# First batch's queries and keys loaded and turned in two token parts, with a new hand-written order, in an attention and channel-mix kernel

## The chip, the cores and the metric

One core of a Trainium2 chip runs the whole kernel in one launch. The metric is the device time of one execution in microseconds (us). A run's time is the time of the whole execution; the profiler's span, from the first to the last instruction, is some 2 us shorter.

## What is computed

Eight batches of 576 tokens. First, attention with 8 heads of 64 dimensions and a causal mask over blocks of 64 tokens; then, on its output `x` (576 tokens by 512 channels), a channel mix:

```
scores = q @ k^T / 8, kept where block(i) >= block(j)      # block = token // 64
x      = softmax(scores) @ v                               # heads side by side: 512 channels
xk     = mu_k * x + (1 - mu_k) * x_prev                    # x_prev: x one token earlier, 0 at the first
xr     = mu_r * x + (1 - mu_r) * x_prev
kk     = max(xk @ w_k, 0)                                  # 512 -> 1024
out    = sigmoid(xr @ w_r) * ((kk * kk) @ w_v)             # 1024 -> 512
```

Inputs and output are float32; the products run in 16 bits with float32 sums.

## The kernel before

**Tasks and order.** The kernel first lists all its work as tasks (`plan.add`): each names its engine, its inputs and the ring buffers that it uses. Then it issues them in the order of a list of task numbers, `ORDER` (line 15). Each engine works through its own tasks in that order and waits where an input isn't there or a buffer isn't free. Where a task may run on several engines, a letter of `PLACE` (line 53) says which: P for GpSimd (POOL), D for VectorE (DVE), A for ScalarE (ACT). A number with `+n` puts n "unread" products ahead of a TensorE (PE) task: 128x512 products whose result nobody reads (`unread`, line 218). A PSUM tile is taken from a ring of four (`ps`), and the queries and keys land in a ring of four tiles (`nb`).

**Queries and keys.** `add_qk` (line 235) loads, for a batch b and a pair half g, the queries (n = 0) or keys (n = 1) of four heads as one 128-partition tile: 288 KB after the conversion to bf16 that the DMA makes. The DMAs are issued from POOL's queue (line 249), two per tile in batches 0 and 1 (64 partitions each), one per tile from batch 2 on. VectorE then turns the tile with one transpose (line 260).

**Scores and exponentials.** `add_unit` (line 349) makes a group of score products `sc` (line 365), 8 to 32 small products of 32 rows by 64 columns, and the exponential of them on ScalarE, `ex` (line 386). In batches 0 and 1 a group is cut in two halves of heads: half 0 needs only g = 0, half 1 only g = 1.

**Batch 0 goes by tokens.** Its scores are made for tokens 0 to 255 (groups "00", "01") and for 256 to 575 ("10" to "14"); `add_part` (line 506) makes for each part the row sums (`sum`, line 524), their reciprocals (lines 405 to 419), the products with the values (`av`, line 544) and the normalised x (`norm`, line 556). The loads of batch 0 are whole all the same: a score of the first part waits for whole tiles.

**Values.** For batch 0 a one-column copy on ScalarE, `hold` (line 293), stands ahead of the loads of the values: it reads the first key tile and writes into the value tile, so that the value loads (line 284, half from SP's queue, half from ACT's) go out only when the first keys have landed. POOL converts the first value tile (line 214), then issues the weights' loads (line 324) and batch 1's queries and keys.

**Mix.** `add_mix` (line 572) makes for each of four channel groups the difference or scaled copy `d` (line 584, or 580 on ScalarE) and from it xk and xr with one VectorE instruction each, `mul` (lines 600 and 604). Then come the products `pk` with w_k (line 644), `pr` with w_r (line 687), `pv` with w_v (line 721), with `relu` and `sq` (lines 659 to 671), `tanh` (line 697), the output `o` (line 731) and its store (line 740). A chunk c is 512 tokens across the batches' borders.

**PE's order in batch 0:** 27 unread products; the seven half-0 score groups of both parts; the two half-1 groups of the first part; its `sum` and `av`; the five half-1 groups of the second part; 9 unread products; `sum` and the two `av` of the second part; then `pr` and `pk` of chunk 0, mixed with batch 1's scores.

Of the kernel before, what the change touches and what calls it, by code (L numbers as in the profile page):

```python
# [8 lines left out]
FP = mybir.dt.float32  # L9
# [3 lines left out]
ALU = mybir.AluOpType  # L13

ORDER = """
# [38 lines left out]
    "DDDDPDPAPADDAPPAADAADPPDDPAPDPAAPPDADAPPPDAADAPDDAPDPDPDPAADPAAAADPAAA"  # L54
    "AAAAADPDADPAADPAPAPAPDDDAADAADPDAAPAAAPADAPADAADPADAA")
# [56 lines left out]
def kernel(  # L112
# [60 lines left out]
    def new(buf):  # L173

        return slots[buf["ring"], buf["slot"]]
# [9 lines left out]
    MUS = consts.tile([P, 2, D], FP)  # L185
    MUT = consts.tile([P, 2, 2, RW], FP)
# [11 lines left out]
    SPLIT = (0, 1)  # L198
    HALVES = (0, 1)
# [35 lines left out]
    def add_qk(b, g, n):  # L235

        src, qkt = (q, k)[n], qkt_buf[b]
        nb = plan.buf("nb")  # L240

        def rows():
            return new(nb)

        def fetch(eng, me):
            parts = ([(D * y, D, GH * y + 2 * g, 2) for y in range(2)]
                     if b in HALVES else [(0, P, GH * g, GH)])
            for p0, np_, h0, nh in parts:
                nc.gpsimd.dma_start(
                    rows()[p0:p0 + np_],  # L250
                    src[b, h0:h0 + nh].rearrange(
                        "y (r j) d -> (y r) (j d)", j=TOK))
        t = add(f"qkld {b} {g} {n}", ("POOL",), fetch, uses=[nb], kind="ldc",
                kb=P * LW * 4 / 1024, starts=2 if b in HALVES else 1)

        if n:
            loads.setdefault(b, (nb, t))

        def turn(eng, me):
            nc.vector.transpose(  # L260
                new(qkt)[:, n, g].rearrange("p t e -> p (t e)").bitcast(
                    FP).rearrange("p (r j) -> p j r", r=RW),
                rows()[:, :].bitcast(FP).rearrange(
                    "p (j s) -> p j s", s=RW))
        evac["qkt", b, g, n] = add(f"turn {b} {g} {n}", ("DVE",), turn, [t],
                                   uses=[nb, qkt], kind="turn", cols=S)

# [70 lines left out]
    PARTS = [(0, 256), (256, 576)]  # L338
# [10 lines left out]
    def add_unit(b, name, pieces, split):  # L349
# [23 lines left out]
        for h in range(2):  # L373
            if split or not h:
                mine = (2 * h, 2 * h + 1) if split else range(GH)
                pe = add(f"sc {b} {name} {h}", ("PE",),
                         lambda eng, me, mine=mine: fn(eng, me, mine),
                         [evac["qkt", b, g, n]
                          for g in sorted({place(b, a, y)[0] for a in mine
                                           for y in range(2)})  # L380
                          for n in range(2)],
                         uses=([ms[h]] if split else ms) + [qkt_buf[b]],
                         kind="sc", cols=[n for _, _, _, n in pieces])
# [188 lines left out]
    def add_mix(b, cc, lo0, hi, xs):  # L572
# [16 lines left out]
        for n in range(2):  # L589
            buf = mix_buf[b][n]  # L590

            def mul(eng, me, n=n, buf=buf):
# [5 lines left out]
                e = nc.vector if eng == "DVE" else nc.gpsimd  # L598
                if sub["eng"] == "ACT":
                    e.scalar_tensor_tensor(  # L600
                        dst, x, MUT[:, n, cc % 2, cc // 2:cc // 2 + 1],
                        dt[:, n, 0:W], ALU.mult, ALU.add)
                else:
                    e.scalar_tensor_tensor(  # L604
                        dst, dt[:, 0, 0:W],
                        MU1[:, n, cc % 2, cc // 2:cc // 2 + 1], x,
                        ALU.mult, ALU.add)
            t = add(f"mul {b} {cc} {n} {lo0}",
                    ("DVE",), mul,
# [139 lines left out]
    add("spare", ("PE",), lambda eng, me: unread(me, new(wbuf)[:, 0]), uses=[wbuf],  # L749
# [84 lines left out]
```

## Time and profile before

| | |
|---|---|
| median of 3 runs | 260.37 us (259.85 to 262.7) |
| the profiled execution's own time | 262.33 us |
| its span | 260.2 us |
| PE busy | 242.6 us, 93% of the span |
| DVE, ACT, POOL busy | 73%, 62%, 31% |
| PE busy from 0 to 62 us | 49.39 us |
| PE busy from 100 to 250 us | 150.0 us |

How to read it. A line such as `L365` is a line of the kernel. In the timeline a row is: start, duration, engine, line, operation, result and source with their shape, count, and in brackets the idle time before it and what ended that. Rows of the same kind are merged, so the duration can contain short waits. "issue" stands for idle time in which the engine waited for nothing that the profile shows. The TensorE clock that was granted is given as a share of full speed. PE's ends are modelled, so a busy PE is not PE at its peak.

### The profile page before, as it was taken

To read this page: it belongs to the slowest core of one execution; us is meant where nothing else is said; L and a number is where in the kernel's file an instruction comes from. 1 tells how busy PE (TensorE), PEld (TensorE's weight loads), DVE (VectorE), ACT (ScalarE), POOL (GpSimd) and SP (SyncE) were. 2 spreads that over 40 slices of the span, in tenths; PEclk is the share of its full clock that TensorE was granted. 3 is DMA by queue.
4 is the path that set the end of the run, shared out by engine and by line. 5 is a ranking of instruction groups with operands and counts; after the bars stand their busy time and mean duration, and the time that the engine had idled before them with its cause. 6 is when DMAs were issued, how large, how long until landed. Compare 5 with 4: busy or idle time off the path is not lost.

```text
span 260.2 us, 8926 instructions
## 1 busy us (share of the span) xinstructions
PE 242.6 (93%) x4058; PEld 132.3 (51%) x4058; DVE 188.8 (73%) x233; ACT 162.4 (62%) x184; POOL 80.3 (31%) x88
## 2 busy tenths in 40 slices
PE   8859498879999999999999999999999999999994
PEld 3536356654454446644454487444554764444442
DVE  1737889597888699899688969884699389444322
ACT  1456048877656969796777786786887743274220
POOL 6074256841405610060455234420000221142000
PEclk9988989997999999999999999999999999999999
DMA  5999996899699995449785930021002200300224
GB/s 88 194 165 189 207 217 103 134 191 215 102 253 238 168 208 181 90 96 215 196 137 97 215 110 3 3 98 65 4 5 81 83 5 12 150 3 0 81 82 161
DMA packets 49189, 31.50 MB, mean 121 GB/s; under 512 B 38528, under 2 KB 39808, under 8 KB 49152
## 3 DMA queue, kind: packets, MB, share of 16 engines
q1 hardware_dynamic: 40128, 18.29, 29.7%
q0 software_dynamic: 6688, 12.06, 27.6%
q10 hardware_dynamic: 2336, 0.59, 1.5%
q8 instruction: 31, 0.51, 0.8%
q14 instruction: 6, 0.05, 0.1%
HBM read 33.56 MB, written 9.44 MB: 165 GB/s over the span
## 4 chain that ended last, share of the span: by engine, by line
PE 84%; DMA 6%; ACT 3%; issue 3%; DVE 1%; POOL 0%; ACTq 0%; DVEq 0%; POOLq 0%
PE t_ps L644 25%; PE t_ps L721 23%; PE t_ps L687 12%; PE t_ps L365 10%; PE t_ps L460 8%; PE t_ps L449 4%; DMA t_lv<-in_v_dram 4%; ACT t_e L386 2%; PE t_ps L544 2%; DMA t_nb<-in_k_dram 1%; DMA out_dram<-t_o 1%; PE t_ps L222 1%; DVE t_o L731 1%; PE t_ps L524 1%; ACT L293 0%
## 5 line engine op out<-in xcount | busy, mean ns | idle before, releaser
L386 ACT ACTIVATE t_e<-t_ps 128x1024 f16<-128x1024 f32 (+4 forms) x98 | 87.6, 957 | 30.9 <-PE t_ps L365 30.1
L644 PE MATMUL t_ps<-t_xk,WK 128*128 128x512 f16 (+3 forms) x416 | 66.9, 314 | 0.4 <-ACT t_e L386 0.3
L721 PE MATMUL t_ps<-WV,t_k 128*128 128x512 f16 (+1 forms) x296 | 64.6, 374 | 0.0
L671 POOL TENSOR_TENSOR t_k<-t_kr 128x1024 f16<-128x1024 f32 x16 | 30.5, 1907 | 76.9 <-DVE t_kr L661 62.5
L644 PEld LDWEIGHTS <-WK 128*128 128x128 f16 x416 | 37.0, 98 | 26.1 <-issue 2.4
L721 PEld LDWEIGHTS <-t_k 128*128 128x128 f16 x296 | 28.1, 98 | 33.1 <-issue 1.9
L365 PE MATMUL t_ps<-t_qkt 32*64 32x64 bf16 (+7 forms) x1344 | 37.3, 290 | 6.1 <-ACT t_e L386 3.8
L260 DVE STREAM_TRANSPOSE t_qkt<-t_nb 128x576 f32<-128x576 f32 x32 | 38.1, 1242 | 1.5 <-PE t_ps L365 1.0
L697 ACT ACTIVATE t_t<-t_ps 128x1024 f32<-128x1024 f32 x18 | 18.5, 1028 | 31.5 <-PE t_ps L687 31.5
L687 PE MATMUL t_ps<-WR,t_xr 128*128 128x512 f16 x144 | 35.1, 390 | 0.4 <-ACT t_e L386 0.4
L659 ACT ACTIVATE t_kr<-t_ps 128x1024 f32<-128x1024 f32 x22 | 22.4, 1024 | 18.8 <-PE t_ps L644 18.3
L365 PEld LDWEIGHTS <-t_qkt 32*64 32x64 bf16 x1344 | 21.8, 106 | 22.9 <-issue 17.9
L731 DVE SCALAR_TENSOR_TENSOR t_o<-t_t,t_ps 128x1024 f32<-128x1024 f32 (+2 forms) x20 | 22.1, 1108 | 14.9 <-PE t_ps L721 9.9
L661 DVE TENSOR_SCALAR t_kr<-t_ps 128x1024 f32<-128x1024 f32 x14 | 17.1, 1224 | 19.5 <-PE t_ps L644 19.4
L584 POOL TENSOR_TENSOR t_d<-t_xt 128x576 f32<-128x576 f32 (+2 forms) x10 | 11.6, 1162 | 36.3 <-DVE t_xk L604 13.5
L687 PEld LDWEIGHTS <-t_xr 128*128 128x128 f16 x144 | 13.7, 100 | 17.2 <-issue 2.5
L460 PE MATMUL t_ps<-t_e,t_vo 64*32 64x512 f16 (+7 forms) x1120 | 21.6, 295 | 0.0
L460 PEld LDWEIGHTS <-t_vo 64*32 64x32 f16 x1120 | 14.9, 95 | 8.8 <-issue 4.5
L604 DVE SCALAR_TENSOR_TENSOR t_xk<-t_d,MU,t_xt 128x576 f16<-128x576 f32 (+2 forms) x24 | 19.2, 802 | 0.1
L497 DVE TENSOR_TENSOR t_xt<-t_ps,t_rt 128x1024 f32<-128x1024 f32 x14 | 16.9, 1218 | 3.2 <-PE t_ps L460 3.1
L580 ACT ACTIVATE t_d<-t_xt,MU 128x576 f32<-128x576 f32 (+1 forms) x24 | 16.8, 751 | 3.7 <-DVE t_xr L604 2.6
L214 POOL CAST t_vo<-t_lv 128x1152 f16<-128x1152 f32 x8 | 9.7, 1216 | 30.5 <-PE t_ps L460 19.3
(40 smaller groups left out, 181.7 us busy)
## 6 DMA issues: line engine op xcount, KB each, us to landing
out_dram<-t_o SPq DMA_DIRECT2D x17, 512.0 KB, 3.3
t_lv<-in_v_dram SPq DMA_DIRECT2D x30, 288.0 KB, 6.3
t_nb<-in_k_dram POOLq DMA_DIRECT2D x12, 288.0 KB, 6.4
t_nb<-in_q_dram POOLq DMA_DIRECT2D x12, 288.0 KB, 6.2
t_nb<-in_k_dram POOLq DMA_DIRECT2D x8, 144.0 KB, 6.3
t_nb<-in_q_dram POOLq DMA_DIRECT2D x8, 144.0 KB, 6.3
WK<-in_moe_w_k_dram POOLq DMA_DIRECT2D x4, 256.0 KB, 6.7
WV<-in_moe_w_v_dram POOLq DMA_DIRECT2D x4, 256.0 KB, 9.0
```

Of the source, the lines that this page charges most:

```text
L260: nc.vector.transpose(new(qkt)[:, n, g].rearrange("p t e -> p (t e)").bitcast(FP).rearrange("p (r j) -> p j r", r=RW), rows()[:, :].bitcas ...
L365: nc.tensor.matmul(new(ms[a // 2])[y * D:y * D + D, a % 2, col:col + n], qkt[rows, 1, g, t * D:t * D + D, f], qkt[rows, 0, g, q0:q0 + n, f ...
L386: nc.scalar.activation(new(e)[:, 2 * h:2 * h + 2, 0:w], new(ms[h])[:, :, 0:w], AF.Exp, scale=ISQ)
L460: nc.tensor.matmul(PA[o, u, HALF + f * D:HALF + f * D + D] if kind == "T" else PA[o, u, lo - D:lo - D + n], weight(b, u, c, t % JT, f), E[ ...
L604: e.scalar_tensor_tensor(dst, dt[:, 0, 0:W], MU1[:, n, cc % 2, cc // 2:cc // 2 + 1], x, ALU.mult, ALU.add)
L644: nc.tensor.matmul(ps[:, x, y * w + a:y * w + a + n], WK[:, cc, jc * P:(jc + 1) * P], MIX[0][:, cc, at:at + n], start=(cc == 0), stop=(cc ...
L659: nc.scalar.activation(kt, ps, AF.Relu, scale=ROOT)
L671: (nc.vector if eng == "DVE" else nc.gpsimd).tensor_tensor(dst, KR, KR, ALU.mult)
L687: nc.tensor.matmul(ps[:, x], MIX[1][:, cc, g:g + P], WR[:, cc], start=(cc == 0), stop=(cc == CCn - 1))
L697: nc.scalar.activation(new(tb), new(m), AF.Tanh, scale=0.5)
L721: nc.tensor.matmul(ps[:, x, cols], k2[:, jc, at:at + P], WV[:, jc, cols], start=(jc == 0), stop=(jc == JCn - 1))
L731: nc.vector.scalar_tensor_tensor(new(o)[:, xs, cols], new(tb)[:, xs, cols], 1.0, new(m)[:, xs, cols], ALU.add, ALU.mult)
```

## The change

- **Loads.** Each of batch 0's four query and key tiles is loaded and turned in two parts, tokens 0 to 255 and 256 to 575. The first parts of all four tiles come first, then the second parts. Batch 0 has 16 DMAs on POOL's queue in place of 8 and 8 transposes in place of 4; batch 1 has one DMA per tile in place of two. A score group of the first part waits for first parts alone; one of the second part waits for the second part of the queries and both parts of the keys.
- **Values.** `hold` reads the first part of the queries of g = 1, the fourth part loaded, in place of the first keys, and in ACT's order it stands behind two exponentials.
- **Unread products.** 15 in place of 27 at the start, in two groups of 10 and 5; later in batch 0 and 1, 7, 3, 5, 3 and 3 in place of 1, 1 and 9. `SHORT` is 0, so its loop makes nothing.
- **Mix.** `mul` may now be placed on POOL too, where it is two instructions, a multiplication into a new buffer `PART` and an addition. The new `PLACE` puts 28 of the 72 there; in batch 0 they are xk and xr of channel group 1, xr of group 2 and both of group 3 for the first part, and three of the second.
- **Order.** `ORDER` is new throughout. PE in batch 0: 15 unread, all four groups of the first part, then the second part's groups, with `sum` of the first part after two of them and `av` of the first part after all of them; then `pk`, `pk`, `pr` of chunk 0 and batch 1. POOL: after the weights two tiles of batch 1, then five `mul` and one `d`, then the other two tiles. The end of the order, from chunk 7's `pk` on, is as before on PE.

The two lists of numbers are left out here, and so are renamings.

```diff
+    PART = consts.tile([P, S], FP)
...
+    PARTS = [(0, 256), (256, 576)]
+    QKP = [[(0, 256), (256, 576)], [(0, 256), (256, 576)]]
...
-    def add_qk(b, g, n):
+    def add_qk(b, g, n, part, nbs):
...
+        lo, hi = QKP[g][part] if b == 0 else (0, S)
+        tok = (hi - lo) // RW
+        c0, c1 = lo // RW * D, hi // RW * D
...
-            parts = ([(D * y, D, GH * y + 2 * g, 2) for y in range(2)]
-                     if b in HALVES else [(0, P, GH * g, GH)])
+            if b in HALVES and hi - lo == S:
+                nc.gpsimd.dma_start(
+                    new(nb),
+                    src[b].rearrange("(y g h) (r j) d -> g y h r (j d)",
+                                     y=2, g=2, j=TOK)[g])
+            elif b in HALVES:
+                for y in range(2):
+                    a = GH * y + 2 * g
+                    nc.gpsimd.dma_start(
+                        new(nb)[y * D:y * D + D, c0:c1],
+                        src[b, a:a + 2, lo:hi].rearrange(
+                            "h (r j) d -> h r (j d)", j=tok))
...
-        if n:
-            loads.setdefault(b, (nb, t))
+        if (b, g, n, part) == (0, 1, 0, 0):
+            loads[b] = (nb, t)
 
         def turn(eng, me):
             nc.vector.transpose(
-                new(qkt)[:, n, g].rearrange("p t e -> p (t e)").bitcast(
-                    FP).rearrange("p (r j) -> p j r", r=RW),
-                rows()[:, :].bitcast(FP).rearrange(
+                new(qkt)[:, n, g, lo:hi].rearrange(
+                    "p t e -> p (t e)").bitcast(FP).rearrange(
+                        "p (r j) -> p j r", r=RW),
+                new(nb)[:, c0:c1].bitcast(FP).rearrange(
                     "p (j s) -> p j s", s=RW))
...
-                          for n in range(2)],
+                          for n in range(2)
+                          for part in ((0,) if b or name[0] == "0" else
+                                       range(len(QKP[g])) if n else
+                                       (len(QKP[g]) - 1,))],
...
+                scaled, r, rest = ((x, rate(MUT), dt[:, n, 0:W])
+                                   if sub["eng"] == "ACT" else
+                                   (dt[:, 0, 0:W], rate(MU1), x))
+                if eng == "DVE":
+                    nc.vector.scalar_tensor_tensor(
+                        dst, scaled, r, rest, ALU.mult, ALU.add)
                 else:
-                    e.scalar_tensor_tensor(
...
+                    nc.gpsimd.tensor_scalar(PART[:, 0:W], scaled, r, None,
+                                            ALU.mult)
+                    nc.gpsimd.tensor_tensor(dst, PART[:, 0:W], rest, ALU.add)
             t = add(f"mul {b} {cc} {n} {lo0}",
-                    ("DVE",), mul,
+                    ("DVE", "POOL"), mul,
...
+    SHORT = 0
+
+    def spare(eng, me):
+        dst, rest = new(wbuf)[:, 0], me["fill"]
+        me["fill"] = min(rest, 10)
+        unread(me, dst)
+        for n in range(SHORT):
...
+        me["fill"] = max(rest - 10, 0)
+        unread(me, dst)
...
     for b in range(B):
-        for g in range(2):
-            for n in range(2):
-                add_qk(b, g, n)
+        nbs = {}
+        for part in range(2 if b == 0 else 1):
+            for g in range(2):
+                if b == 0 and part >= len(QKP[g]):
+                    continue
+                for n in range(2):
+                    add_qk(b, g, n, part, nbs)
```

More of the change, by code (lines that the diff above doesn't have):

```diff
@@ L231 @@
     xt_buf = [plan.buf("xt") for _ in range(B)]
-    def add_qk(b, g, n):
+    def add_qk(b, g, n, part, nbs):
         src, qkt = (q, k)[n], qkt_buf[b]
-        nb = plan.buf("nb")
-        def rows():
-            return new(nb)
+        if (g, n) not in nbs:
+            nbs[g, n] = plan.buf("nb")
+        nb = nbs[g, n]
+        lo, hi = QKP[g][part] if b == 0 else (0, S)
+        tok = (hi - lo) // RW
+        c0, c1 = lo // RW * D, hi // RW * D
+        name = f"{b} {g} {n}" + (f" {part}" if b == 0 else "")
@@ L256, in add_qk @@
-        if n:
-            loads.setdefault(b, (nb, t))
+                    new(nb),
[8 more added lines that the diff above has]
+                            "h (r j) d -> h r (j d)", j=tok))
+            else:
+                nc.gpsimd.dma_start(
+                    new(nb), src[b, GH * g:GH * g + GH].rearrange(
+                        "y (r j) d -> (y r) (j d)", j=TOK))
@@ L259, in turn @@
+        t = add(f"qkld {name}", ("POOL",), fetch, uses=[nb], kind="ldc",
+                kb=P * D * (hi - lo) // RW * 4 / 1024,
+                starts=1 + (b in HALVES and hi - lo < S))
+        if (b, g, n, part) == (0, 1, 0, 0):
+            loads[b] = (nb, t)
         def turn(eng, me):
             nc.vector.transpose(
-                new(qkt)[:, n, g].rearrange("p t e -> p (t e)").bitcast(
-                    FP).rearrange("p (r j) -> p j r", r=RW),
-                rows()[:, :].bitcast(FP).rearrange(
+                new(qkt)[:, n, g, lo:hi].rearrange(
+                    "p t e -> p (t e)").bitcast(FP).rearrange(
+                        "p (r j) -> p j r", r=RW),
+                new(nb)[:, c0:c1].bitcast(FP).rearrange(
@@ L264, in turn @@
                     "p (j s) -> p j s", s=RW))
-        evac["qkt", b, g, n] = add(f"turn {b} {g} {n}", ("DVE",), turn, [t],
-                                   uses=[nb, qkt], kind="turn", cols=S)
+        evac["qkt", b, g, n, part] = add(
+            f"turn {name}", ("DVE",), turn, [t], uses=[nb, qkt], kind="turn",
+            cols=hi - lo)
     def place(b, a, y):
@@ L337 @@
     ]
-    PARTS = [(0, 256), (256, 576)]
     PIECES = [
@@ L747 @@
     wbuf = plan.buf("ps")
-    add("spare", ("PE",), lambda eng, me: unread(me, new(wbuf)[:, 0]), uses=[wbuf],
+    SHORT = 0
[4 more added lines that the diff above has]
+        for n in range(SHORT):
+            at = n % GH * RW
+            nc.tensor.matmul(dst[at:at + RW, 0:D], identb[:, 0:RW],
+                             identb[:, 0:D], start=True, stop=True)
+        me["fill"] = max(rest - 10, 0)
+        unread(me, dst)
+    add("spare", ("PE",), spare, uses=[wbuf],
         kind="spare", cols=[])
```

22 lines of the change are left out of this document (6 added, 16 removed), and 70 rows, old and new, of the table ORDER.

## The prediction

> **What bounds the kernel now.** I read the busy time by stretches first, then the chain of waits over the first 60 us, then PE's own timeline there, and the other engines' timelines to see what the changed start could meet. The stretches (length, then busy time of PE, its weight loads, DVE, ACT, POOL; the granted clock, the DMA share and GB/s):
>
> ```profile
> 0.00:62.00 62.00, 49.39 (x1074) 30.72 (x1082) 43.41 (x71) 34.29 (x42) 30.11 (x47) 0.92 1.00 168
> 62.00:89.50 27.50, 26.15 (x470) 12.93 (x470) 21.96 (x25) 19.34 (x21) 10.57 (x10) 0.99 1.05 203
> 89.50:251.40 161.90, 161.90 (x2499) 85.68 (x2498) 120.81 (x134) 106.68 (x120) 39.63 (x32) 1.00 0.38 89
> ```
>
> From 89.5 us on PE is never idle, and the change removes no product there: a gain can only come from the 62 − 49.39 = 12.6 us and the 27.5 − 26.15 = 1.35 us that PE idles before, and from the clock, granted at 0.92 there. The last 9 us are the output's tail, the same in both.
>
> The chain says what ends last in the start:
>
> ```profile
> 1.94 3.31 DMA t_nb<-in_k_dram
> 7.59 9.27 DMA t_lv<-in_v_dram
> 18.23 0.41 issue
> 24.52 0.51 PE t_ps L524 x9
> 25.03 0.09 issue
> 27.52 3.79 issue
> ```
>
> So it is first keys (landed at 1.94 + 3.31 = 5.25), then values, and then three stalls called "issue": PE waits for no semaphore. PE's timeline and the DMA queues tell what these are:
>
> ```profile
> 9.61 2.59 PE L365 MATMUL t_ps<-t_qkt 32*64 32x256 bf16 x104 [0.95 <-DVE t_qkt L260]
> ...
> 18.64 0.73 PE L544 MATMUL t_ps<-t_e,t_vo 64*32 64x256 f16 x30 [0.39 <-issue]
> 19.30 3.17 PE L365 MATMUL t_ps<-t_qkt 32*64 32x320 bf16 x80
> 22.41 2.12 PE L222 MATMUL t_ps<-identb 128*128 128x512 bf16 x9
> 24.45 1.53 PE L524 MATMUL t_ps<-t_e,pick 128*32 128x320 f16 x40
> 25.92 1.60 PE L544 MATMUL t_ps<-t_e,t_vo 64*32 64x320 f16 x97
> 31.31 1.21 PE L544 MATMUL t_ps<-t_e,t_vo 64*32 64x320 f16 x63 [3.79 <-issue]
> ```
> ```profile
> PE 242.6 (93%) x4058; PEld 132.3 (51%) x4058; DVE 188.8 (73%) x233; ACT 162.4 (62%) x184; POOL 80.3 (31%) x88
> ...
> q8 instruction: 31, 0.51, 0.8%
> ...
> t_nb<-in_k_dram POOLq DMA_DIRECT2D x12, 288.0 KB, 6.4
> ```
>
> From the stall before 18.64 to the one before 25.12 stand 30 + 80 + 9 + 9 = 128 products, from there to 31.31 stand 40 − 9 + 97 = 128 again. The queue named "instruction" carried 31 packets for 4058 products, one per 131. So PE's program comes in blocks of about 128 products, each by one DMA packet, and in the start PE executes blocks faster than they come. The laps are 25.12 − 18.64 = 6.5 us and 31.31 − 25.12 = 6.2 us. The block before begins 128 products ahead of 18.64, at the 67th of the 104 score products, at about 9.61 + 67 × 2.59/104 = 11.3, an estimate: a lap of 7.3 us. This sets the second part's `av`, hence everything up to 32.5 us. An earlier first score helps only as far as it starts these laps earlier.
>
> After 32.5 the bound is ScalarE:
>
> ```profile
> 32.45 3.20 PE L687 MATMUL t_ps<-WR,t_xr 128*128 128x512 f16 x8
> 47.02 1.89 PE L687 MATMUL t_ps<-WR,t_xr 128*128 128x512 f16 x8 [0.44 <-ACT t_e L386]
> 35.69 1.02 ACT L697 ACTIVATE t_t<-t_ps 128x1024 f32<-128x1024 f32 x1 [11.12 <-PE t_ps L687]
> 42.60 6.80 ACT L386 ACTIVATE t_e<-t_ps 128x1024 f16<-128x1024 f32 x8 [0.81 <-ACT t_e L386]
> 52.86 1.94 ACT L386 ACTIVATE t_e<-t_ps 128x1024 f16<-128x1024 f32 x2 [1.50 <-PE t_ps L365]
> ```
>
> The same eight products took 3.20 us in the first row and 1.89 in the second: after the 3.79 us stall the clock was low. Batch 2's first exponential starts at 52.86.
>
> **The start, term by term.** These rows price the loads, turns and the first ScalarE work:
>
> ```profile
> 1.00 7.66 PE L222 MATMUL t_ps<-identb 128*128 128x512 bf16 x27 [1.00 <-DVE identb L178]
> 1.24 1.23 POOL L249 DMA_DIRECT2D t_nb<-in_k_dram  x2 [0.79 <-POOLq L818]
> 4.39 3.78 PEld L222 LDWEIGHTS <-identb 128*128 128x128 bf16 x18 [0.28 <-issue]
> 4.48 1.09 POOL L249 DMA_DIRECT2D t_nb<-in_q_dram  x2
> 5.32 1.28 ACT L293 ACT_TABLE_LOAD   x1 [5.32 <-DMA t_nb<-in_k_dram]
> 6.84 2.23 ACTq L284 DMA_DIRECT2D t_lv<-in_v_dram  x2
> 11.21 1.26 DVE L260 STREAM_TRANSPOSE t_qkt<-t_nb 128x576 f32<-128x576 f32 x1 [0.45 <-DMA t_nb<-in_q_dram]
> ```
>
> Four whole tiles landed between 5.25 and 11.2, about 2.0 us each. A first part is 256/576 of a tile, 0.9 us by the bytes; but POOL needs about 1.08 us to issue a pair ((4.48 + 1.09 − 1.24)/4), so the first parts come at POOL's pace. The first one lands at 5.25 less at most 1.1 us; I take 4.5, then 5.6, 6.7, 7.7. Second parts (1.1 us by bytes, 1.08 by issue) land at about 8.8, 9.9, 11.0 and 12.1: the last data come 0.9 us later than now. Turns: 1.26 × 256/576 = 0.56 and 0.70 us. The first score can run at 5.6 + 0.56 = 6.2. The unread products end at 4.39 + 7 × 0.21 = 5.9, eight of the 15 being done by 4.39: the twelve removed lay beside waiting and are worth nothing by themselves, and counting the later ones 36 stand for 38. The Trainium skill speaks against parts: its page "DMA: Bandwidth & Descriptors", section "Anatomy of one DMA", gives each DMA a fixed cost of about 2.0 us beside bytes/436 GB/s, so that sixteen small ones would pay it twice as often; one 64 KB part would land about 2.2 us after its issue, an estimate. The trace's first pair of 144 KB took 5.25 − 1.24 = 4.0 us, and fixed costs overlap where the next one is issued 0.54 us later: by that rule the first landing would be 3.4 instead of my 4.5, and the rest stays at POOL's pace.
>
> The first block border comes after 94 products counted from the start (27 + 67). In the new order that is the sixth product of the second part's first group (15 + 16 + 16 + 23 + 16 + 3 = 89 stand ahead). That group needs the second part of the first queries: 9.9 + 0.70 = 10.6. If PE's sequencer reads ahead while it waits, the request leaves once the waits of the group before end, at about 8.5 (7.7 + 0.56 behind `mu1`). So the border moves from 11.3 to between 8.5 and 10.6; I take 9.8, **−1.5 us**, bounds −0.7 and −2.8. The three laps stay as long as DMA is as busy; the values now go out behind two exponentials at about 8.4 instead of 6.84, which shifts that traffic, not its amount: they land at 16.9 + 1.6 = 18.5, before the first part's `av` asks (it now stands behind all score groups). On SP only later values queue behind them; on POOL the first values' conversion, and behind it the weights, slip by as much, to some 26 with 6.4 us to land, and `pk` asks at 31. ACT's two value issues (2.23 us) now delay the third exponential; the laps cover this, and without them it would cost up to 2.2 us. The table load ahead of `hold` is not tied to data that I can see; if it waits with the first exponential it costs 1.28 us, under the same cover. In the last lap 56 instead of 64 products follow: **−0.15**. The second part's `av` then ends at 32.5 − 1.65 = 30.9.
>
> From there to batch 2's first exponential the kernel before takes 52.86 − 32.5 = 20.4 us. Now `pk`, `pk` and `pr` follow (1.89 us each at full clock, all three of as many columns: 5.7), `tanh` 1.02, then ScalarE runs without a gap: 12 exponentials of 0.85 (6.80/8), a `relu` and a `tanh` of 1.02: 12.2 us; `relu`, `sq` and `d` hide under the `pr`. Sum 19.0: **−1.4**, and 0 if the clock is low as in the first L687 row (+1.3).
>
> Next, the new order puts three groups of batch 1's `av` and three of batch 2's scores in a stretch with no large product (`av` A, B, S and T, 327 small products against 224 before). That is 0.8 of a block more in a row, where laps decide. Bounds: 0 (ScalarE covers it, 8 exponentials last 6.8 us) to a whole stall like the 3.79; I take **+0.6**, near the cover.
>
> The rest (batch 3 on) I put at **0**: PE is full, and only 1.35 us idle is left to win. Sum −1.5 − 0.15 − 1.4 + 0.6 = −2.45, rounded −2.5. The profiled execution took 262.33 us (span 260.2), 0.8% above the median 260.37; the sum holds for either: 259.8 for that execution, **257.9 us** for the median.
>
> **The 28 multiplications on POOL** take 28 off VectorE, which isn't the bound, and stand in POOL's queue ahead of loads:
>
> ```profile
> L584 POOL TENSOR_TENSOR t_d<-t_xt 128x576 f32<-128x576 f32 x7 | 9.4, 1343 | 32.0 <-DVE t_xk L604 13.5 <-DVE t_xr L604 8.5 <-DVE t_xk L600 5.8
> L604 DVE SCALAR_TENSOR_TENSOR t_xk<-t_d,MU,t_xt 128x576 f16<-128x576 f32 x17 | 15.4, 911 | 0.1
> 22.22 0.48 DVE L604 SCALAR_TENSOR_TENSOR t_xk<-t_d,MU,t_xt 128x256 f16<-128x256 f32 x1
> 23.52 0.78 POOL L584 TENSOR_TENSOR t_d<-t_xt 128x256 f32<-128x256 f32 x1 [3.58 <-DVE t_xr L604]
> 23.75 0.84 DVE L604 SCALAR_TENSOR_TENSOR t_xk<-t_d,MU,t_xt 128x256 f16<-128x256 f32 x1
> 25.31 1.07 POOL L249 DMA_DIRECT2D t_nb<-in_k_dram  x2
> ```
>
> Two passes of 1343 ns replace one of 911, at 256 columns two of 0.78 replace 0.48. Beside POOL's pass VectorE's instruction took 0.84 instead of 0.48: the two engines slow each other. `pk` of chunk 0 needs the fifth POOL job of the first part: from about 22.6 (an estimate: the first part's `av` now ends the block that ends at 25.12 − 1.5 = 23.6, and normalisation and a difference follow it) 4 × 2 × 0.78 + 0.78 = 7.0 us, done at 29.6, 1.3 us before PE asks. Then the g = 1 loads of batch 1 go out at 31.2 instead of 25.31; ScalarE wants them after four of the first exponentials, at 30.9 + 5.7 + 1.0 + 4 × 0.85 = 41, and 31.2 + 6.4 + two turns of 1.26 is 40.1. So I cost this at nothing, with 1.3 us of cover.
>
> **Rivals.**
> - *Slower: POOL's passes.* If a pass over 256 columns takes more than about (30.9 − 22.6)/9 = 0.92 us, POOL and not PE's blocks decides. At 0.78 × 0.84/0.48 = 1.37 us nine passes end at 34.9, +4.0, and batch 1's second loads slip with them to 37.6; ready at 46.5, where ScalarE, 4.0 later too, wants them at 45: +5.5 in all. Net +1.5 to +3: 261.9 to 263.4 us. For it: the 0.84 row. Against: 1.3 us of cover, and one row only. The Trainium skill, page "GPSIMD Engine Reference", section "Specifications", says that POOL's interface to SBUF is shared with VectorE and contended by VectorE's instructions with two SBUF inputs, which `mul` and `d` have; this trace's 0.84 us against 0.48 agrees.
> - *Gain: the stalls go.* If the border at 8.5 puts the request ahead of the values' traffic, the first lap shrinks and the 0.41 + 3.79 us stalls go with it: −2.5 less another 3.8, near 254 us. For it: values now go out later. Against: the later laps, of 6.5 and 6.2 us, fell in weight and batch 1 traffic that is unchanged.
> - *No change.* The earlier border is given back in the stretch without large products, 3.79 instead of 0.6, or at the low clock: 259.4 to 261.
>
> **How the numbers follow.** Chances: forecast (256.4 to 259.4) 0.42, slower 0.22, larger gain 0.17, no change 0.19. One per cent, 2.6 us, is about what a measurement of this kernel can tell from no change. The forecast lies at that edge: 0.24 of its 0.42 lie below 257.8. So faster 0.24 + 0.17 = 0.41, same 0.18 + 0.19 = 0.37, slower 0.22. The range 254.2 to 262.6 leaves out half of the larger gain (0.08) and half of the slower case (0.11), 0.2.
>
> **What would show it.** The first L365 row near 6.2; the stalls "issue" still 128 products apart, the large one ending near 30; batch 2's first exponential near 49.5; POOL's new passes at 0.8 us for 256 columns and 1.3 for 576; no idle PE from 90 us on. I am wrong if the laps change length, if L644's first row waits for POOL, or if PE idles after 90 us.

## The result, and the profile after

The change made the kernel slower: 284.75 us median of four runs (283.31 to 286.6), against 261.19 (259.85 to 262.7) for the kernel before. The ratio is 1.091, with a 95% interval of 1.086 to 1.096. The forecast was 257.9 us with a range of 254.2 to 262.6. Below, a run's time is the median of all its executions, and its ratio to the kernel before, measured beside it, leaves out executions more than 1.5% above the fastest of the same kernel.

The busy time by stretches, cut where the prediction cut it for the kernel before (same columns), then PE's line and the queues of the page:

```profile
0.00:62.00 62.00, 39.27 (x667) 24.14 (x668) 25.59 (x50) 21.30 (x29) 38.05 (x53) 0.75 0.83 115
62.00:89.50 27.50, 24.84 (x487) 13.91 (x486) 22.95 (x24) 19.32 (x22) 19.19 (x21) 0.88 1.07 178
89.50:276.00 186.50, 182.24 (x2877) 96.01 (x2876) 137.76 (x142) 120.95 (x133) 96.69 (x66) 1.00 0.44 99
```
```profile
PE 251.3 (88%) x4056; PEld 136.9 (48%) x4056; DVE 189.0 (66%) x218; ACT 163.4 (57%) x183; POOL 153.9 (54%) x138
...
q0 software_dynamic: 18016, 12.11, 29.0%
```

The span grew from 260.2 to 284.8 us, by 24.6. Two parts make it up. PE idles 284.8 − 251.3 = 33.5 us in place of 260.2 − 242.6 = 17.6: 15.9 us more, of which 10.1 in the first 62 us (22.7 against 12.6). And nearly the same products (4056 and 4058) cost 251.3 − 242.6 = 8.7 us more busy time; the granted clock was 0.75 and 0.88 in the first two stretches in place of 0.92 and 0.99. After 89.5 us PE, never idle before, idles 4.3 us. The queue of POOL's loads moved the same bytes in 18016 packets; before it was

```profile
q0 software_dynamic: 6688, 12.06, 27.6%
```

What PE waited for in the whole span (us, times, longest), after and then before:

```profile
PE t_ps L383 <- DVE t_qkt L277: 13.8, 3, 8.5
PE t_ps L668 <- POOL t_xk L631: 2.4, 1, 2.4
```
```profile
PE t_ps L365 <- DVE t_qkt L260: 1.0, 1, 1.0
```

Scores wait 12.8 us longer for turned queries and keys. The chain of waits after says what stands behind that (start, length, what), and the timelines of PE, DVE and POOL show it from their sides:

```profile
2.80 6.31 DMA t_nb<-in_q_dram
...
12.84 10.46 DMA t_nb<-in_q_dram
...
42.98 14.29 DMA t_nb<-in_k_dram
```
```profile
10.72 1.28 PE L383 MATMUL t_ps<-t_qkt 32*64 32x256 bf16 x32 [3.62 <-DVE t_qkt L277]
...
18.98 1.10 PE L383 MATMUL t_ps<-t_qkt 32*64 32x320 bf16 x40 [1.70 <-DVE t_qkt L277]
...
32.44 1.74 PE L565 MATMUL t_ps<-t_e,t_vo 64*32 64x320 f16 x105
36.83 0.97 PE L565 MATMUL t_ps<-t_e,t_vo 64*32 64x320 f16 x55 [2.65 <-issue]
...
56.65 5.26 PE L383 MATMUL t_ps<-t_qkt 32*64 32x512 bf16 x88 [8.51 <-DVE t_qkt L277]
```
```profile
23.39 0.74 DVE L277 STREAM_TRANSPOSE t_qkt<-t_nb 128x320 f32<-128x320 f32 x1 [2.91 <-DMA t_nb<-in_q_dram]
...
53.14 1.26 DVE L277 STREAM_TRANSPOSE t_qkt<-t_nb 128x576 f32<-128x576 f32 x1 [9.76 <-DMA t_nb<-in_k_dram]
```
```profile
29.77 0.90 POOL L254 DMA_DIRECT2D t_nb<-in_k_dram  x1
...
32.89 1.08 POOL L629 TENSOR_SCALAR PART<-t_d,MU 128x256 f32<-128x256 f32 x1 [1.40 <-DVE t_d L605]
...
42.98 0.89 POOL L254 DMA_DIRECT2D t_nb<-in_k_dram  x1
```

The first score runs at 10.72 us (forecast 6.2), the last second part is turned at 23.39 (forecast: landed by 12.1), and batch 1's first tile, issued at 29.77, is turned at 53.14. In its first 58 us the chain now runs through loads of queries and keys and through 10 us of POOL's work ahead of the last of them, and no longer through values and blocks.

### The profile page after: what moved, and what is told of

Same layout as the page of the kernel before. It is cut to its first block, busy times and chain, and to the rows that moved or that the text cites. A ratio compares the mean times of both kernels' runs of the same rounds, so it can differ in the third digit from the quotient of the medians.

```text
span 284.8 us, 8971 instructions
## 1 busy us (share of the span) xinstructions
PE 251.3 (88%) x4056; PEld 136.9 (48%) x4056; DVE 189.0 (66%) x218; ACT 163.4 (57%) x183; POOL 153.9 (54%) x138
## 3 DMA queue, kind: packets, MB, share of 16 engines
q0 software_dynamic: 18016, 12.11, 29.0%
## 4 chain that ended last, share of the span: by engine, by line
PE 63%; DMA 15%; DVE 10%; POOL 5%; ACT 3%; issue 3%; DVEq 0%; POOLq 0%
PE t_ps L745 20%; PE t_ps L668 19%; DMA t_nb<-in_q_dram 9%; PE t_ps L711 8%; PE t_ps L481 7%; PE t_ps L383 6%; DMA t_nb<-in_k_dram 5%; PE t_ps L470 3%; ACT t_e L407 2%; DVE t_o L755 2%; POOL PART L629 2%; POOL t_nb L261 2%; DVE t_qkt L277 1%; DVE t_xk L626 1%; DVE t_xr L626 1%
## 5 line engine op out<-in xcount | busy, mean ns | idle before, releaser
L407 ACT ACTIVATE t_e<-t_ps 128x1024 f16<-128x1024 f32 (+3 forms) x98 | 87.4, 958 | 55.0 <-PE t_ps L383 49.8
L383 PE MATMUL t_ps<-t_qkt 32*64 32x64 bf16 (+7 forms) x1344 | 41.5, 308 | 20.5 <-DVE t_qkt L277 13.8
L277 DVE STREAM_TRANSPOSE t_qkt<-t_nb 128x576 f32<-128x576 f32 (+2 forms) x36 | 39.3, 1121 | 29.0 <-DMA t_nb<-in_k_dram 20.3
L695 POOL TENSOR_TENSOR t_k<-t_kr 128x1024 f16<-128x1024 f32 x12 | 22.7, 1897 | 44.0 <-ACT t_kr L683 39.5
L629 POOL TENSOR_SCALAR PART<-t_d,MU 128x576 f32<-128x576 f32 (+2 forms) x20 | 35.1, 1753 | 18.9 <-DVE t_d L605 16.5
L383 PEld LDWEIGHTS <-t_qkt 32*64 32x64 bf16 x1344 | 25.3, 114 | 38.6 <-issue 25.8
L683 ACT ACTIVATE t_kr<-t_ps 128x1024 f32<-128x1024 f32 x26 | 26.6, 1022 | 23.9 <-PE t_ps L668 23.9
L755 DVE SCALAR_TENSOR_TENSOR t_o<-t_t,t_ps 128x1024 f32<-128x1024 f32 (+2 forms) x20 | 22.1, 1110 | 20.9 <-PE t_ps L745 10.1
L481 PE MATMUL t_ps<-t_e,t_vo 64*32 64x512 f16 (+7 forms) x1120 | 22.6, 295 | 2.0 <-DVE t_tt L426 1.3
L605 DVE TENSOR_TENSOR t_d<-t_xt 128x576 f32<-128x576 f32 (+2 forms) x21 | 17.0, 822 | 4.0 <-POOL PART L629 3.7
L685 DVE TENSOR_SCALAR t_kr<-t_ps 128x1024 f32<-128x1024 f32 x10 | 12.2, 1222 | 10.1 <-PE t_ps L668 10.1
L693 ACT ACTIVATE t_k<-t_kr 128x1024 f16<-128x1024 f32 x15 | 15.9, 1057 | 3.5 <-DVE t_kr L685 3.1
## 6 DMA issues: line engine op xcount, KB each, us to landing
t_lv<-in_v_dram ACTq DMA_DIRECT2D x2, 288.0 KB, 12.1
WR<-in_moe_w_r_dram POOLq DMA_DIRECT2D x2, 256.0 KB, 11.3
```

The lines of the kernel that those rows point to most:

```text
L277: nc.vector.transpose(new(qkt)[:, n, g, lo:hi].rearrange("p t e -> p (t e)").bitcast(FP).rearrange("p (r j) -> p j r", r=RW), new(nb)[:, c ...
L383: nc.tensor.matmul(new(ms[a // 2])[y * D:y * D + D, a % 2, col:col + n], qkt[rows, 1, g, t * D:t * D + D, f], qkt[rows, 0, g, q0:q0 + n, f ...
L407: nc.scalar.activation(new(e)[:, 2 * h:2 * h + 2, 0:w], new(ms[h])[:, :, 0:w], AF.Exp, scale=ISQ)
L481: nc.tensor.matmul(PA[o, u, HALF + f * D:HALF + f * D + D] if kind == "T" else PA[o, u, lo - D:lo - D + n], weight(b, u, c, t % JT, f), E[ ...
L629: nc.gpsimd.tensor_scalar(PART[:, 0:W], scaled, r, None, ALU.mult)
L683: nc.scalar.activation(kt, ps, AF.Relu, scale=ROOT)
```

## The experiments

Two causes were set against each other at first. **S**: the new loads land late because of their form. Their source is walked as two heads, then 32 rows of a head; the kernel before merged both into 64 rows. **P**: POOL's multiplications stand ahead of loads and of `pk`. Later a third was added, **O**: the new order itself. The rows for S, from the views of landings (KB of each DMA, median us from issue to landing; after, then `r11_flat_mul_dve` below, with the same bytes in 64 rows):

```profile
t_nb<-in_k_dram POOLq DMA_DIRECT2D x4, 64.0 KB, 6.0
```
```profile
t_nb<-in_k_dram POOLq DMA_DIRECT2D x4, 64.0 KB, 2.4
```

**Batch 1's tiles by two merged DMAs again (r1), and the reverse edit alone on the kernel before (r4).**

```diff
 # r1, on the changed kernel (r4: the same two forms exchanged, in the kernel before)
-                nc.gpsimd.dma_start(
-                    new(nb),
-                    src[b].rearrange("(y g h) (r j) d -> g y h r (j d)",
-                                     y=2, g=2, j=TOK)[g])
+                for y in range(2):
+                    a = GH * y + 2 * g
+                    nc.gpsimd.dma_start(
+                        new(nb)[y * D:y * D + D],
+                        src[b, a:a + 2].rearrange("h (r j) d -> (h r) (j d)", j=TOK))
```

> The changed kernel, with batch 1's four query and key tiles loaded by two DMAs each, in the form of the kernel before (the rows of two heads merged into one outermost dimension of 64). Theory S (spread: a DMA whose source has an outermost dimension of 2 runs on few of the 16 DMA engines): a tile lands in about 6 us in place of the 14.3 us that the chain shows from 42.98, the two waits of batch 1 shrink, and the kernel comes to 270 to 277 us. Theory P (POOL's multiplications ahead of the loads in its queue are what costs): the loads go out no earlier, 281 to 285 us.

> The kernel before, with only batch 1's four tiles loaded by one DMA each, in the form of the changed kernel (outermost source dimension 2). Theory S: each lands some 14 us after its issue in place of 6.3, the last one, issued near 28, near 42, so that batch 1's second half of scores starts some 4 us later; 264 to 270 us. Theory P: nothing changes but four issues fewer, 260 to 262 us.

r1: 279.36 us, ratio 1.071 (1.065 to 1.077): 2.0 of the 9.1% of loss, some 5 us, less than S had expected of it. r4: 268.08 us against 260.21 beside it, 1.031 (1.026 to 1.035), inside S's range: this one edit, four DMAs fewer, costs 8 us by itself. Its chain:

```profile
18.52 21.39 DMA t_nb<-in_k_dram
```

In r4 batch 1's four tiles land 17.8 to 21.4 us after their issue. In the kernel before, the halves of these same tiles took 8.8 us (keys) and 6.9 us (queries), medians, beside the same weights; the queries' row is

```profile
t_nb<-in_q_dram POOLq DMA_DIRECT2D x4, 144.0 KB, 6.9
```

In the changed kernel the landings of the line that issues these tiles are

```profile
DMA to landing us min/median/max: 13.8/18.8/24.0
```

and while such tiles are on their way there, the DMA engines are about half used (last two columns: share, GB/s):

```profile
46.00:56.00 10.00, 2.14 (x10) 0.91 (x9) 2.86 (x3) 2.08 (x4) 3.69 (x5) 0.74 0.57 97
```

The Trainium skill, page "DMA: Bandwidth & Descriptors", section "Why a DMA increments its semaphore by 16 and not by 1", has a rule for this: a DMA runs on the largest number of engines, up to 16, that divides the slowest dimension of both its sides. With two heads outermost that is two engines per DMA, with 64 merged rows 16; four tiles on their way would use eight of sixteen, which the share of 0.57 agrees with. The packet records of the same trace agree too. Of the 2304-byte packets that carry these tiles, 4 are in flight at once from 43 to 44.5 us, with two tiles on their way, and 7 to 9 from 48 to 53 us, with four; from 57 us on, when a tile of batch 2 with merged rows is on its way, it is 17. One packet lasts 0.19 us (median) in both cases. So the packets are not slower, fewer run at a time: 128 of them on two engines make 64 × 0.19 = 12.2 us, an estimate, where the shortest landing is 13.8.

**All loads as before, order and multiplications of the change (r3); also all multiplications on VectorE (r6); after with the multiplications alone moved (r5).**

```diff
 # r3: batch 1 as in r1; batch 0's second parts load and turn nothing, the first ones the whole tile
-                for y in range(2):
+                for y in range(2 if part == 0 else 0):
 # r5 (after) and r6 (r3): in the planner
+                if t["info"].get("kind") == "mul":
+                    t["eng"] = "DVE"
```

> The changed kernel with all loads as in the kernel before: batch 0's tiles whole (with the first part's task, the second part's task loads nothing) and turned whole, batch 1's by two DMAs. The new order, the multiplications on POOL and the late value loads stay. Theory S: most of the 23.6 us goes, 260 to 267 us. Theory P: 273 us or more.

> The changed kernel with all 72 multiplications on VectorE; its loads stay in the new forms. Theory S: POOL issues batch 1's second pair of tiles some 8 us earlier, which helps, but they still land 14 us later: 274 to 281 us. Theory P: 260 to 267 us.

> The changed kernel with all loads as in the kernel before (batch 0 whole, batch 1 by two DMAs) and all 72 multiplications on VectorE: of the change only the new order, the late value loads and the unread products are left. Theory S+P (the loads' form and POOL's multiplications together make the loss): 259 to 264 us. Theory O (the order itself is slower): 267 us or more, within 3 us of the 273.2 us with the multiplications on POOL.

r3: 273.18 us, 1.052 (1.047 to 1.057), where S alone had expected 267 at most. r5: 284.43 us, 1.094 (1.088 to 1.100): no gain at all, which misses P's range and S's. r6: 271.64 us, 1.042 (1.035 to 1.049), in O's range. So the new form of the loads is some 43% of the loss (9.1 to 5.2%), the new order with its late values costs 4.2% here, and P as stated, the multiplications ahead of batch 1's second pair, falls: in r5 POOL issues that pair at 33.52 instead of 42.98 us, and PE waits for turned tiles even longer (17.4 us in all, 13.8 in after), since the first pair lands late too. Its POOL row, and PE's wait:

```profile
33.52 0.82 POOL L256 DMA_DIRECT2D t_nb<-in_k_dram  x1
```
```profile
PE t_ps L385 <- DVE t_qkt L279: 17.4, 3, 10.3
```

**r3 with batch 1's second pair issued ahead of POOL's first six mix instructions (r9).** Only places in the order move.

> As the kernel with all loads in the old form (273.2 us, multiplications on POOL), but batch 1's second pair of tiles is issued ahead of POOL's first six mix instructions instead of behind them. If POOL's multiplications cost through the loads that stand behind them: those go out near 28 in place of 38.1, and the kernel comes to 262 to 267 us. If they cost through their own lateness (chunk 0's products wait for POOL) or through the order: 269 to 274 us.

276.1 us, 1.058 (1.053 to 1.062), outside both ranges and not faster than r3; the two intervals overlap. The pair's place behind the multiplications is not what costs. The rows show what the move does instead. On POOL the issue of a load waits, by the profile, for the landing of weights issued earlier, and the multiplications stand behind that issue. In r3:

```profile
27.54 0.52 POOL L256 DMA_DIRECT2D t_nb<-in_q_dram  x1 [3.36 <-DMA WK<-in_moe_w_k_dram]
28.18 0.94 POOL L634 TENSOR_SCALAR PART<-t_d,MU 128x256 f32<-128x256 f32 x1
```

In r9 four more such issues come first, the multiplications begin at 33.71 in place of 28.18, and `pk` waits 5.3 us for POOL, where it waited 1.0 in r3.

**The 28 multiplications on POOL in the kernel before (r12).** The change's two POOL instructions, for the same 28, in the order of before.

> The kernel before, its order and loads untouched, with the same 28 multiplications placed on POOL as two instructions each. Theory P: three of them stand ahead of batch 1's first load and the others ahead of later ones, each pair of passes about 1.6 us at 256 columns and 3 to 4 at 576; 265 to 275 us. If POOL's passes are hidden here: 259 to 262 us.

274.6 us, 1.052 (1.048 to 1.056), inside P's range. In an order not laid out for them they cost nearly 14 us. What PE waits for after 90 us, and that stretch (of 174 us PE is busy 165.68; before it idled nowhere there):

```profile
PE t_ps L680 <- POOL t_xk L643: 6.8, 3, 2.9
```
```profile
90.00:264.00 174.00, 165.68 (x2524) 86.47 (x2500) 116.79 (x117) 107.66 (x121) 100.79 (x69) 0.98 0.36 86
```

**Parts in other forms: head by head (r7), and from one contiguous stretch (r10), the latter with the multiplications on VectorE (r11).** Batch 1 as in r1. r7 gives each part four DMAs with 32 rows outermost. r10 and r11 fetch a part's bytes from 2 × 256 or 2 × 320 tokens that lie together, so 64 rows are outermost: batch 0 reads other tokens than it should, and only the times are of use; bytes, counts and order are those of the change.

```diff
 # r10, r11
-                        src[b, a:a + 2, lo:hi].rearrange(
-                            "h (r j) d -> h r (j d)", j=tok))
+                        src[b, a:a + 2].rearrange("h s d -> (h s) d")[
+                            2 * lo:2 * hi].rearrange("(p j) d -> p (j d)", j=tok))
```

> The changed kernel with batch 1 by two DMAs per tile, and batch 0's parts loaded head by head: 32 DMAs of 32 partitions, whose outermost dimension is 32, in place of 16 of 64 partitions with an outermost dimension of 2. Theory S: the data come at POOL's issue pace (some 0.54 us each), the first four parts by about 11.5, the last near 20, no later than with few engines; 273 to 279 us against 279.4. If the count of DMAs is what costs: above 280 us.

> The changed kernel with batch 1 by two DMAs per tile, and each part of batch 0 fetched from one contiguous stretch of the input in place of two heads' token ranges: the same 16 DMAs, bytes, turns and order, but an outermost source dimension of 64. (It reads other tokens than it should, so batch 0's result is not the reference's.) This is the change as the prediction understood it. By the prediction's sum, with POOL's multiplications at the measured 1.64 us: first parts turned from about 5 us on, the first block border near 10, 256 to 263 us. Theory O (the order loses some 10 us even where the parts land early, as the kernel with whole tiles did): 266 to 272 us.

> The same, with all 72 multiplications on VectorE as well. If POOL's multiplications cost little beside this order (1.5 us with whole tiles): within 3 us of the run before. If they hold back batch 1's loads now that the start is earlier: 4 to 8 us less, 253 to 259 us.

r7: 277.45 us, 1.064 (1.059 to 1.068), inside S's range. A DMA of 32 KB lands in 2.2 us, but POOL issues 32 of them, four in about 2.0 us, until 20 us. r10: 272.68 us, 1.042 (1.033 to 1.052): the change as the prediction understood it is still slower, by some 11 us, about what O had expected. r11: 269.18 us, 1.031 (1.025 to 1.038). PE's rows of r11, and the row of its first exponential of batch 1:

```profile
6.27 0.76 PE L388 MATMUL t_ps<-t_qkt 32*64 32x256 bf16 x32 [0.16 <-DVE t_qkt L282]
...
11.12 1.10 PE L388 MATMUL t_ps<-t_qkt 32*64 32x320 bf16 x40 [0.69 <-DVE t_qkt L282]
...
30.73 0.79 PE L570 MATMUL t_ps<-t_e,t_vo 64*32 64x320 f16 x55 [3.23 <-issue]
...
32.98 6.06 PE L673 MATMUL t_ps<-t_xk,WK 128*128 128x256 f16 x29 [0.97 <-DVE t_xk L631]
38.88 1.89 PE L716 MATMUL t_ps<-WR,t_xr 128*128 128x512 f16 x8
...
41.56 2.45 PE L388 MATMUL t_ps<-t_qkt 32*64 32x512 bf16 x64 [0.15 <-DVE t_qkt L282]
```
```profile
42.26 6.20 ACT L412 ACTIVATE t_e<-t_ps 128x1024 f16<-128x1024 f32 x7 [0.43 <-PE t_ps L388]
```

The first score is where the forecast had it (6.2), and the second part's `av` ends at 30.73 + 0.79 = 31.5 (30.9). But 29 `pk` products take 6.06 us, where 16 took 1.89 at full clock by the prediction (the granted clock was 0.50 from 33 to 37 us), and batch 1's scores begin at 41.56. Nor do all loads land on time: the first four parts do, the last second part does not. VectorE turns it at 17.16 after waiting for its DMA, 5 us after the 12.1 of the forecast, and the first part's row sums, which PE waits for to be read, stand behind it:

```profile
17.16 0.74 DVE L282 STREAM_TRANSPOSE t_qkt<-t_nb 128x320 f32<-128x320 f32 x1 [2.92 <-DMA t_nb<-in_q_dram]
17.75 0.40 DVE L431 STREAM_TRANSPOSE t_tt<-t_ps 128x256 f32<-128x256 f32 x1
```

The values go out at 8.40, right when these second parts are on their way. The chain shows the values' road:

```profile
8.40 10.39 DMA t_lv<-in_v_dram
...
18.92 1.14 POOL t_vo L220
...
24.23 12.86 DMA t_nb<-in_k_dram
```

**15 unread products in the kernel before (r13).** Only the number in the first word of the order changes, 27 to 15.

> The kernel before with 15 unread products at the start in place of 27, nothing else. As predicted, the twelve lie beside waiting: 259.5 to 262 us. If they keep the clock up for batch 0's first scores, or move the block borders for the worse: 263 us or more; if fewer products bring the borders forward: 258 us or less.

261.54 us, 1.0005 (0.997 to 1.004): no difference, as forecast.

**Late values, and what else the order holds (r14 to r17).** r14 is r11 with the values sent out early, r15 also puts `pk 0 4 0` behind four scores, r16 is r14 with the 28 multiplications on POOL; r17 is the kernel before with values late.

```diff
 # r14, r15, r16 (r17 the other way, on the kernel before), with hold and its DMAs moved in the order
-        if (b, g, n, part) == (0, 1, 0, 0):
+        if (b, g, n, part) == (0, 0, 1, 0):
             loads[b] = (nb, t)
```

> r11_flat_mul_dve (269.2 us: parts fetched from one contiguous stretch, batch 1's tiles by two DMAs, all multiplications on VectorE) with the values sent out as before: ScalarE's two copies wait for the first of the four first key parts and stand ahead of the first exponential, and the values' DMAs right behind them. Theory V, that the late values delay POOL's cast, the weights' loads behind it and the first normalizing: issue at 6 to 7 us instead of 8.4 (SyncE) and 8.4 to 11.0 (ScalarE), VectorE's cast of the values at 17 instead of 20.8 as before, first norm at 19 to 20 instead of 23.6, batch 1's first exponential 40 or earlier instead of 42.3, total 263 to 266. Rival, the order of PE's and VectorE's work itself: VectorE's cast earlier but the total within 2 us of r11, 267.5 to 270.

> r14_early with the second block of 16 key products (pk 0 4 0), its relu and its square behind batch 1's first four score products, where the kernel before has them. If the order of these products is what holds batch 1 back, its first exponential comes 2 to 3 us earlier than in r14 (16 products took 1.9 us at full clock and 3.0 at the low one) and the total falls by 2 to 3 us; if late values were all, no more than 1 us either way.

> r14_early with the 28 multiplications left on POOL as the change has them, that is the change as it was predicted but with early values. r10 to r11 put their price at 3.5 us. If that holds: r14 plus 2 to 4.5, 265 to 270. If POOL's passes cost only because the late values had filled POOL's queue: r14 plus 0 to 1.

> The kernel before with the values late: ScalarE's two copies wait for the fourth whole load (landing about 10.8) instead of the first (5.3) and stand with the values' DMAs behind the first two exponentials. Theory V: issue at 12 to 13 us, landing 18 to 20, VectorE's cast of the values about 21, the first norm near 23.5 instead of 19.5, total 264 to 268. Rival, that values have slack: 260 to 262.

r17: 263.54 us, 1.010 (1.008 to 1.013): late values cost 2.3 to 2.7 us in the order of before, less than V had expected and more than its rival. r14: 269.95 us, 1.028 (1.021 to 1.036): in the new order early values win nothing clear of noise; V's range is missed, and the rival's, the order itself, holds. r16: 272.5 us, 1.042 (1.035 to 1.048). Two rows of r16 say why early values don't help there: its first score group of the second part, and a wait by `pk`.

```profile
13.61 1.29 PE L386 MATMUL t_ps<-t_qkt 32*64 32x320 bf16 x40 [3.23 <-DVE t_qkt L280]
```
```profile
PE t_ps L671 <- POOL t_xk L634: 2.7, 1, 2.7
```

That group starts at 13.61 after waiting 3.23 us; in r11 it started at 11.12 after 0.69. So with the values ahead the second parts come later: the wait has moved. r15: 274.98 us against 261.21, 4 to 5 us worse than r14 and without an interval of its own, where 2 to 3 us of gain were expected of it; that `pk` stands ahead of batch 1's scores is not the cause either.

**What remains.** By the ratios the way from after back to before reads: the form of batch 1's loads 2.0% (1.091 to 1.071, some 5 us), the form of batch 0's parts 2.9% (to 1.042, 7.5 us), the multiplications on POOL 1.1% (to 1.031, 3 us), and 3.1% (8 us) of order, which neither r14 nor r15 removes. The 1.1 is not sure by itself, since the intervals of r10 and r11 overlap; the same step was 1.0% from r3 to r6, 1.3% from r16 to r14, and nothing from after to r5. And parts as such may be worth something when they land early: r10 is 1.0% below r3 and r11 1.0% below r6, which load whole tiles, though these intervals overlap too. Where the 8 us lie in r11 its profile tells:

```profile
0.00:62.00 62.00, 48.11 (x1000) 30.73 (x1006) 40.55 (x72) 34.92 (x44) 33.45 (x54) 0.92 0.94 158
62.00:89.50 27.50, 23.71 (x418) 12.25 (x418) 24.62 (x26) 17.58 (x20) 11.11 (x11) 0.94 0.86 172
89.50:258.50 169.00, 166.82 (x2618) 88.02 (x2616) 130.17 (x146) 108.89 (x120) 24.17 (x22) 1.00 0.40 94
```
```profile
PE t_ps L388 <- DVE t_tt L431: 3.5, 1, 3.5
PE t_ps L388 <- DVE t_o L760: 3.5, 2, 2.0
```

PE idles 1.3 us more than before in the first stretch, 2.4 more in the second and 2.2 in the third, and is busy for 1.0 more in the whole span. Two waits on VectorE, 3.5 us each, are new: the one for `t_tt` comes from the late second part above, the one for `t_o` falls between 60 and 100 us. VectorE carries 28 multiplications here in an order laid out for POOL, and its first normalizing comes at 23.56 in place of 19.50. So the order's loss looks like several small waits that replace one another when one is taken out; that is argued from these rows, not shown by a run that removes them. Which part of the order would have to change to lose them stays open.

## Why the prediction was wrong

- **The step that failed first: "A first part is 256/576 of a tile, 0.9 us by the bytes", hence landings at POOL's pace, 4.5 to 7.7 us for the first parts and 12.1 for the last second part.** I costed the parts by bytes and by POOL's issue and didn't weigh the changed order of the source's dimensions, which the diff shows. The first turns came at 7.7 to 12.6 us, the last second part at 23.39. POOL's pace slipped as well, to some 1.35 us a pair, with waits for earlier landings in between. With merged rows (r11) the first four parts landed as forecast and the first score came at 6.27; the last second part was 5 us late even there. I weighed the fixed cost of a DMA, on the Trainium skill's page "DMA: Bandwidth & Descriptors", and passed over the rule of the same page that is shown with r4.
- **The same failure, unstated: batch 1's one DMA per tile.** I used 6.4 us to land for it. Landings took 13.8 to 24.0 us; by r4 this alone costs 8 us.
- **"−1.5 us" at the first block border** was too good even with loads on time: in r11 the group that holds the border starts at 11.12, 0.5 later than my bound for it, so the border did not move ahead of the estimated 11.3. The count of a block held: the stall "issue" stands 105 products into the second part's `av` in after, r11 and r16 alike. The length of the laps did not: from the border, six products into that group, to the end of the large stall the three laps took 30.73 − 11.3 = 19.4 us in r11 and 36.83 − 19.1 = 17.7 in after, against 31.31 − 11.3 = 20.0 before.
- **"−1.4" from there to batch 2's first exponential** failed too: its first 6.7 us (`pk`, `pk`, `pr` and `tanh`) were 42.26 − 31.5 = 10.8 in r11. `pk` ran late and at half the clock; `pr` ran at its 1.89 us. The rival of a low clock allowed for 1.3 us of this. The "+0.6" for the stretch without large products is in no run by itself.
- **The values "land at 16.9 + 1.6 = 18.5, before the first part's `av` asks"**: 8.40 + 10.39 = 18.8 in r11, so the time was right; that nothing waits for it was wrong. POOL's cast came at 18.92, the weights behind it, and the first of batch 1's tiles behind those took 12.86 us. Batch 1's scores began at 41.56, where I had them by 36.6 (30.9 + 5.7). ACT's two issues took 4.76 us in after, where I had 2.23; what that costs is not shown, since the next score group waits for turned queries.
- **The rest at 0, since "PE is full",** failed: 4.3 us idle after 89.5 us in after, 8.3 in r12 after 90. Work moved to a slower place makes new idle time where there was none.
- **The slower rival** (POOL's passes, +1.5 to +3) names an engine that does hold PE up: `pk` waits 2.4 us for POOL in after and 2.7 in r16, and r16 is 1.3% above r14. But its reason was another. A `mul` of 256 columns is two passes of 0.92 and 0.72 us with gaps of 0.1, on the mean below the 0.92 that it needed, and the nine passes to `pk`'s fourth group took 8.0 us in after (32.89 to 40.91), where I had 7.0. What was wrong is their start: 32.89 in after and 28.18 in r3, not 22.6, behind the cast of late values, the weights and loads that wait for them. That the sum comes out near is luck. The pass over 576 columns was mis-sized as well: the mean over all forms of the first pass, 1753 ns, already exceeds the 1343 that I used for 576. The page's group, then POOL's timeline in after:

```profile
L629 POOL TENSOR_SCALAR PART<-t_d,MU 128x576 f32<-128x576 f32 (+2 forms) x20 | 35.1, 1753 | 18.9 <-DVE t_d L605 16.5
```
```profile
40.19 0.72 POOL L631 TENSOR_TENSOR t_xk<-PART,t_xt 128x256 f16<-128x256 f32 x1
41.01 0.92 POOL L629 TENSOR_SCALAR PART<-t_d,MU 128x256 f32<-128x256 f32 x1
```

- **Right:** the twelve unread products are worth nothing (r13), the table load is not tied to data (it ran at 0.73 us), and the signs of being wrong that it named: the laps changed length, `pk` waited for POOL, and PE idled after 90 us.

## What to carry to other kernels

Before a load is split or two are merged, write down the outermost dimension of both sides of its access pattern and compare the landing times of the two forms: here an outermost dimension of two instead of 64 cost some 12 us, twice what the forecast's larger gain would have won (6.3 us). When the bound engine is full except for its start, look for what a new order makes late later on, above all behind the queue that carries loads, casts and arithmetic together. And a part's price belongs to the order around it: the same 28 multiplications on POOL cost nearly 14 us in the old order and 0 to 3.5 in the new one, so an edit is priced alone in the old kernel and taken out of the new one before it is kept or blamed.

## What the runs showed of the hardware

- A DMA whose source has two rows outermost takes 2 to 3 times as long to land as the same bytes with 64 merged rows: 17.8 to 21.4 us in r4 against 6.9 to 8.8 before for batch 1's tiles, 6.0 against 2.4 for 64 KB. Two of its packets are in flight at once per tile, 8 for four tiles, where a tile with merged rows has 17. The packets of the queue rise from 6688 to 18016 at nearly the same bytes, to 7328 in r11. POOL's issue of a whole tile in one DMA takes up to 0.90 us, where one of the two before took about 0.54.
- The loss shows twice at TensorE: as waiting and as clock. Granted clock 0.75 in the first 62 us in place of 0.92, 8.7 us more busy time in the whole span for nearly the same products.
- The stall at a block's border stays at the same product when the time before it moves by 6 us (36.83 against 30.73), so its place follows the program and not the time.
- By the profile, a load's issue on POOL can wait for the landing of a DMA issued earlier, and POOL's arithmetic behind it waits too: 3.36 us for a part of the weights in r3. What sets that limit is not shown.
